# Bucketed attention and a gated expert block on one core: hash masks of 15 of 16 head pairs fetched by bucket number

## Chip, core and metric

One Trainium2 chip, one core. The time is device microseconds of one execution of the whole kernel; the median of the runs shown is given beside the profiled execution's own time.

## Reference

```
q_bits = (einsum('bhsd,dk->bhsk', q, proj) > 0)      # 4 x 8 heads, 768 rows, 64 wide; 6 bits a row
k_bits = (einsum('bhsd,dk->bhsk', k, proj) > 0)
mask   = q_bucket[..., :, None] == k_bucket[..., None, :]   # bucket = the number made of the 6 bits
scores = where(mask, q @ k.T / sqrt(64), -1e9)
attn   = softmax(scores)
x      = (attn @ v), heads side by side: 3072 x 512
out    = (sigmoid(x @ w_gate) * (x @ w_val)) @ w_out        # 512 -> 1536 -> 512
```

A query row attends to those keys of its head whose six hash bits are the same as its own.

## The kernel before

Two heads of one batch make a pair; 16 pairs come one after another (`pair`, `group`). Heads lie on partitions 0 to 63 and 64 to 127, and most products of this stage use the two halves of TensorE's rows side by side. For each pair:

- q and k are loaded by rows, transposed by TensorE (tk, tq), and split into a high and a low fp32r part (`high`, `low`: kh, kl, qh, ql). A copy of the q parts with its halves swapped (qsh, qsl) is made by DMA (`swapped`), so that both heads' queries meet both halves.
- The hash (`hash_`, `hashed`, L1370) multiplies k and q by the projection, six full-array products each (hk, hq). `bits_k` and `bits_q` make 0/1 or large values of the signs: six bits and their six complements a row, in bf16 (kb, qb).
- `group` handles 384 queries of both heads, in three chunks of 128 (t) by two heads (h), so 192 score groups in all. `scores` (L1448, L1454) adds up in PSUM first the bits product qb x kb, two products, which is at least 2^34 smaller wherever a bit differs, and then six products of the q and k parts. The scores are negated, so `maximum` (L1466) is one VectorE reduction that evicts PSUM into the buffer e and keeps the minimum of each row. `exponent` (ScalarE, L1475) makes the exponentials and their sums.
- `turned` transposes e back through TensorE (tp, L1508), `whole` copies it into e again (ScalarE or VectorE, L1514), `values` multiplies by v (pv, L1524), `divided` and `store` finish and write x to DRAM.

Between these pieces run the preparation of the expert weights (`load_w`, `load_pair`: VectorE, ScalarE and GpSimd make high and low parts; SyncE keeps them in DRAM) and the first two of twelve blocks of the expert layer for batches whose attention is done (`moe_early`: zg, zv at L897, zo at L933). When all attention is stored, a switch exchanges the buffers, and the expert stage (`products`) does the rest with weights streamed back by GpSimd's queue.

PSUM has three double banks ("two") for scores, transposes and hashes and two single banks; SBUF has three e buffers. The order is not left to the program text: every step is a task with an engine, a cost in ns, and buffers that it takes and gives (`Plan.add`). For TensorE the table ORDER lists the tasks' numbers in the order in which they are issued; on the other engines the task with the least key goes first among those that are ready, and SHIFT moves the keys. A simulation of the plan with those costs fixes every queue before the kernel is built.

```
    def scores(t, h):
...
            for j, rows in enumerate(halves):
                nc.tensor.matmul(
                    sc[:, j, :GN], z["qb"][rows, c], z["kb"][rows, h], start=True, stop=False, tile_position=(j * D, 0),
                )
```

Of the kernel before, what the change touches and what calls it, by code (L numbers as in the profile page):

```python
# [19 lines left out]
P = 128  # L20
# [5 lines left out]
NEVER = 3.0e38  # L26

# [23 lines left out]
    2, 3, 4, 5, 6, 7, 8, 9, 10, 11, 12, 13, 38, 14, 15, 16, 17, 18, 41, 19, 20, 21, 47, 44, 50, 22, 23, 24, 235, 25,  # L51
    26, 27, 53, 55, 59, 28, 61, 65, 67, 94, 243, 96, 29, 30, 74, 100, 76, 102, 106, 78, 108, 86, 137, 80, 82, 87,
    88, 140, 115, 117, 89, 90, 84, 119, 121, 31, 145, 148, 127, 91, 123, 151, 153, 157, 159, 163, 128, 165, 192,
    194, 198, 125, 129, 172, 238, 174, 130, 131, 200, 176, 204, 206, 178, 333, 132, 184, 185, 336, 213, 246, 341,
    344, 186, 249, 180, 251, 255, 257, 261, 263, 225, 187, 182, 215, 217, 188, 189, 226, 219, 270, 272, 227, 274,
    290, 221, 292, 296, 276, 223, 282, 298, 278, 302, 304, 280, 431, 228, 283, 229, 230, 311, 347, 434, 313, 284,
    285, 315, 349, 353, 355, 359, 442, 439, 361, 317, 323, 324, 286, 325, 287, 368, 388, 319, 370, 380, 390, 321,
    394, 396, 372, 400, 402, 374, 376, 381, 326, 382, 327, 383, 328, 409, 378, 445, 447, 451, 453, 457, 384, 421,
    385, 411, 413, 459, 486, 488, 422, 423, 466, 492, 468, 494, 478, 470, 529, 532, 479, 480, 415, 498, 417, 500,
    419, 472, 424, 425, 426, 481, 507, 627, 509, 1924, 1925, 537, 1926, 1927, 540, 1929, 1930, 635, 1931, 1932, 511,  # L60
    474, 543, 545, 630, 519, 520, 482, 521, 513, 549, 476, 551, 555, 515, 517, 483, 522, 523, 524, 557, 584, 586,
    590, 592, 1934, 1935, 1936, 1937, 638, 1941, 1942, 1943, 564, 566, 596, 598, 568, 576, 570, 641, 572, 1944, 725,
    728, 643, 577, 578, 579, 580, 605, 574, 647, 1948, 607, 649, 653, 655, 1949, 733, 736, 1952, 1953, 609, 662,
    664, 617, 581, 618, 619, 666, 682, 611, 684, 688, 690, 694, 696, 1969, 1970, 1971, 1972, 668, 613, 921, 620,
    621, 615, 703, 705, 1974, 1975, 1976, 1977, 929, 1956, 1957, 707, 709, 711, 622, 715, 716, 674, 717, 713, 670,
    739, 741, 745, 747, 751, 675, 718, 719, 720, 753, 780, 782, 672, 1979, 1980, 1981, 1982, 760, 762, 786, 1986,
    1987, 1988, 1989, 764, 788, 766, 792, 794, 768, 770, 676, 677, 678, 679, 823, 801, 826, 1993, 1994, 831, 1997,
    834, 1998, 803, 805, 807, 813, 809, 837, 811, 839, 843, 845, 849, 851, 924, 814, 815, 816, 817, 818, 858, 878,
    860, 862, 870, 871, 864, 880, 884, 886, 890, 892, 2001, 932, 2002, 866, 868, 1019, 872, 772, 873, 773, 874, 774,
    875, 899, 901, 935, 937, 941, 943, 775, 776, 777, 903, 905, 947, 949, 976, 978, 911, 912, 907, 956, 958, 913,  # L70
    914, 960, 962, 964, 968, 909, 966, 982, 984, 988, 969, 970, 971, 915, 916, 972, 973, 990, 1022, 1117, 2014,
    2015, 2016, 2017, 1027, 2019, 2020, 2021, 2022, 1030, 2024, 1125, 2025, 2026, 2027, 1120, 1033, 1035, 2031,
    2032, 2033, 2034, 1128, 2038, 997, 999, 1039, 1001, 1009, 1003, 1041, 1005, 1007, 2039, 1045, 1047, 1074, 1076,
    1080, 2059, 2060, 2061, 2062, 1054, 1082, 1086, 1088, 1056, 2042, 2043, 1215, 1058, 1218, 1010, 1011, 1012,
# [1595 lines left out]
```

## Time and profile before

| | us |
|---|---|
| median of 3 runs (989.72 to 992.89) | 992.26 |
| the profiled execution's own time | 991.96 |
| its span, first to last instruction | 990.1 |
| TensorE busy in the span | 980.5 |
| VectorE busy | 648.8 |
| ScalarE busy | 546.7 |
| GpSimd busy | 184.7 |
| moved by DMA | 195.96 MB |

Busy times are sums over the whole span, which has two very different stages; the rows below are therefore taken by stage where they can be. TensorE's matmuls are pipelined, so its busy time is no proof that it runs at its peak; the chain of waits tells how long each of its groups took in its place.

### The profile page before, as it was taken

The numbers are of one execution on the slowest core, as the hardware profiler recorded it, in microseconds if no ns is written. First come the engines' busy times: TensorE is split into PE (matmuls) and PEld (weight loads), VectorE is DVE, ScalarE is ACT, GpSimd is POOL, SyncE is SP. The second block draws the span as 40 slices with busy tenths as digits, with TensorE's granted clock in tenths as the row PEclk, the third lists the DMA queues.
The fourth block names the chain that finished last, engine by engine and source line by source line (L and its number), as shares of the span: only waits on it lengthen the run. The fifth ranks groups of instructions, "written<-read, shape, count | busy, mean of one in ns | idle before, by whom it ended". The sixth has DMA issues, their size and how long they took to land.

```text
span 990.1 us, 20196 instructions
## 1 busy us (share of the span) xinstructions
PE 980.5 (99%) x8157; PEld 807.4 (82%) x8160; DVE 648.8 (66%) x1254; ACT 546.7 (55%) x1004; POOL 184.7 (19%) x214
## 2 busy tenths in 40 slices
PE   9999999999998999999999999999999999999998
PEld 5676677777677766776789999999999999999997
DVE  7898989878987888988454775643336433553334
ACT  5768878877767777767645443533234333433331
POOL 1001254343344434341111000000000000000000
PEclk9999999999999999999999999999999999999999
DMA  5375396658686748772279976674447644476421
GB/s 129 92 196 146 122 249 186 196 187 243 196 222 179 242 172 250 216 211 92 66 264 390 385 259 234 236 267 174 180 177 254 237 149 159 170 275 225 149 75 64
DMA packets 115853, 195.96 MB, mean 198 GB/s; under 512 B 62640, under 2 KB 85424, under 8 KB 110640
## 3 DMA queue, kind: packets, MB, share of 16 engines
q1 hardware_dynamic: 107568, 120.68, 40.3%
q0 software_dynamic: 5824, 73.41, 19.9%
q8 instruction: 64, 1.05, 0.4%
q10 hardware_dynamic: 2368, 0.59, 0.3%
q14 instruction: 29, 0.24, 0.1%
HBM read 140.91 MB, written 41.94 MB: 185 GB/s over the span
## 4 chain that ended last, share of the span: by engine, by line
PE 96%; DMA 2%; DVE 1%; ACT 0%; SPq 0%; issue 0%; ACTq 0%; DVEq 0%
PE y L933 17%; PE pv L1524 13%; PE sc L1454 10%; PE zBv L1153 8%; PE zBg L1153 8%; PE tp L1508 8%; PE zDv L1153 4%; PE zDg L1153 4%; PE sc L1448 4%; PE zv L897 4%; PE zo L933 3%; PE zg L897 3%; PE zAg L1153 2%; PE zAv L1153 2%; PE hq L1370 2%; PE hk L1370 1%
## 5 line engine op out<-in xcount | busy, mean ns | idle before, releaser
L1475 ACT ACTIVATE e<-e,st 128x768 f32<-128x768 f32 x192 | 178.8, 933 | 32.4 <-DVE e L1466 31.9
L1466 DVE TENSOR_SCALAR_CACHE_REDUCE e<-sc 128x768 f32<-128x768 f32 x192 | 175.8, 952 | 19.0 <-PE sc L1454 17.2
L933 PE MATMUL y<-wo,gh 128*128 128x512 f32 (+1 forms) x484 | 151.1, 394 | 0.0
L1524 PE MATMUL pv<-e,vr 128*64 128x384 f32 x768 | 137.7, 494 | 0.0
L1514 ACT COPY e<-tp 128x768 f32<-128x768 f32 x126 | 99.1, 798 | 38.2 <-PE tp L1508 37.5
L1508 PEld LDWEIGHTS tp<-ident,e 64*128 64x128 f32 x2304 | 84.6, 139 | 36.6 <-issue 13.9
L933 PEld LDWEIGHTS y<-wo,gh 128*128 128x128 f32 x484 | 90.4, 187 | 15.2
L1508 PE MATMUL tp<-ident,e 64*128 64x64 f32 x2304 | 96.8, 226 | 0.0
L1153 PE MATMUL zBv<-x,wsv 128*128 128x384 f32 x480 | 96.4, 335 | 0.0
L1153 PE MATMUL zBg<-x,wsg 128*128 128x384 f32 x480 | 96.3, 335 | 0.0
L1524 PEld LDWEIGHTS pv<-e,vr 128*64 128x64 f32 x768 | 49.2, 136 | 55.2 <-issue 47.6
L933 PE MATMUL y<-wo,gl 128*128 128x512 f32 (+1 forms) x242 | 93.6, 387 | 0.0
L1454 PE MATMUL sc<-kh,qsl 64*128 64x384 f32 x192 | 89.9, 468 | 2.6 <-DMA qsl<-ql 2.5
L1454 PE MATMUL sc<-kh,ql 64*128 64x384 f32 x192 | 90.0, 469 | 0.0
L1153 PEld LDWEIGHTS zBv<-x,wsv 128*128 128x128 f32 x480 | 85.4, 188 | 5.4 <-ACT t16v L1161 0.2
L1153 PEld LDWEIGHTS zBg<-x,wsg 128*128 128x128 f32 x480 | 85.5, 188 | 5.2
L1246 ACT CAST gh<-zt 128x384 fp32r<-128x384 f32 x80 | 41.0, 514 | 85.8 <-DVE zt L1241 67.6
L1514 DVE COPY e<-tp 128x768 f32<-128x768 f32 x66 | 62.0, 950 | 17.6 <-PE tp L1508 17.3
L1448 PE MATMUL sc<-kb,qb 64*128 64x384 bf16 x384 | 65.0, 328 | 0.1
L1454 PE MATMUL sc<-kl,qh 64*128 64x384 f32 x192 | 64.4, 335 | 0.0
L1454 PE MATMUL sc<-kh,qh 64*128 64x384 f32 x192 | 64.3, 335 | 0.0
L1454 PE MATMUL sc<-kh,qsh 64*128 64x384 f32 x192 | 64.2, 334 | 0.0
(182 smaller groups left out, 1965.7 us busy)
## 6 DMA issues: line engine op xcount, KB each, us to landing
wsg<-kzg POOLq DMA_DIRECT2D x20, 1792.0 KB, 7.8
wsv<-kzv POOLq DMA_DIRECT2D x20, 1792.0 KB, 7.6
kzg<-wkg SPq DMA_DIRECT2D x10, 896.0 KB
kzv<-wkv SPq DMA_DIRECT2D x10, 896.0 KB
vr<-in_v_dram SPq DMA_DIRECT2D x16, 384.0 KB
rb<-rd SPq DMA_DIRECT2D x64, 96.0 KB
xd<-xs SPq DMA_DIRECT2D x32, 192.0 KB
rawg<-in_moe_w_gate_dram SPq DMA_DIRECT2D x12, 512.0 KB
```

The costliest lines, as they stand in the source:

```text
L897: nc.tensor.matmul(z["acc"][:, :GN], a[:, wc], x[xx][:, c, :], start=(c == 0 and i == 0), stop=(c == KC - 1 and i == 2),)
L933: nc.tensor.matmul(acc, a[:, slot, ts_], w, start=(first and i == 0), stop=(last and i == 2), skip_group_check=cols != slice(None),)
L1153: nc.tensor.matmul(acc, streams[n, jp][:, c, wa, a_], X[x_][:, xa, c], start=first and c == 0 and i == 0, stop=c == 1 and i == 2, skip_gro ...
L1246: nc.scalar.copy(side["h"][:, blk], w["z", blk])
L1370: nc.tensor.matmul(acc[:, j, :GN], hw[w][a], z[n + x][:, j * GN : (j + 1) * GN], start=m == 0, stop=m == 2,)
L1448: nc.tensor.matmul(sc[:, j, :GN], z["qb"][rows, c], z["kb"][rows, h], start=True, stop=False, tile_position=(j * D, 0),)
L1454: nc.tensor.matmul(sc[:, j, :GN], q_[rows, c], z["k" + x][rows, h * GN : (h + 1) * GN], start=False, stop=(m == 2), tile_position=(j * D, 0),)
L1466: nc.vector.tensor_scalar(sp(e), gz["sc", t, h][:, :, :GN], -MASKED * SCALE, None, op0=ALU.min, op1=ALU.min, accum_out=gz["st", t][:, h : ...
L1475: nc.scalar.activation(e, e, AF.Exp, bias=st[:, h : h + 1], scale=-1.0, accum_out=gz["su"][:, h * GT + t : h * GT + t + 1],)
L1508: nc.tensor.transpose(tp[:, r, at_ : at_ + D], gz["e", t, h][rows, c * P : (c + 1) * P], ident[rows, rows], tile_position=(r * D, 0),)
L1514: copy(gz["e"][:, :, c * P : (c + 1) * P].rearrange("p n (r d) -> p r n d", r=2), gz["tp", c][:, :, :GN].rearrange("p r (n d) -> p r n d", ...
L1524: nc.tensor.matmul(gz["pv"][rows, :GN], z["v"][:, h, c], gz["e"][:, h * GT : (h + 1) * GT, c * P : (c + 1) * P], start=(c == 0), stop=(c = ...
```

## The change

For all pairs but the first, the bits product leaves the score groups. Instead:

- `bits` makes the 12 sign bits of k, and `differ` multiplies them by a table `code` of all 64 bucket numbers (built once from `blank`, `digits`, `code_turned`, `coded`): four bf16 products per pair give, for each of 64 buckets and each key of a head, how many bits differ. `masks` turns this into 0 or 2^60 in bf16, and `keep_masks` writes it to DRAM: 128 rows (two heads by 64 buckets) of 768.
- `hash_q` computes the six hash values of each query with queries on the partitions (24 small products: a 128-query weight and 12 or 6 columns), and `buckets` turns them into a bucket number by three small VectorE instructions.
- `gather`, an indirect DMA on GpSimd's queue, fetches for each query row the mask row of its bucket, into the upper half of that chunk's place in e: 12 per pair, 180 in all, 196,608 bytes each. The six gathers of a group now take the e buffer.
- `maximum` becomes a reduction with two inputs (scores from PSUM, mask from SBUF), which adds and keeps the minimum.
- hash bits of the first pair, its bits product and its reduction stay as they were.
- ORDER and SHIFT are new tables; one line of each:

```
-    2, 3, 4, 5, 6, 7, 8, 9, 10, 11, 12, 13, 38, 14, 15, 16, 17, 18, 41, 19, 20, 21, 47, 44, 50, 22, 23, 24, 235, 25,
+    7, 8, 9, 10, 11, 12, 13, 14, 15, 16, 17, 18, 43, 19, 20, 21, 22, 46, 23, 52, 49, 24, 5, 25, 55, 26, 27, 142, 58,
```

```diff
+DIRECT = (0,)
...
+    GATHER, GATHERED, AHEAD, EARLY = 1250, 5200, 8, 4
...
+        def bits():
+            z["kb"] = at.tile([P, 2, GN], BF16, name=f"kb{u}", tag="kb", bufs=1)
+            nc.vector.tensor_scalar(z["kb"], z["hs", "k"][:, :, :GN], own, None, op0=ALU.is_gt)
+
+        def differ():
+            for h in range(2):
+                for j, rows in enumerate(halves):
+                    nc.tensor.matmul(
+                        z["hs", "k"][:, j, :GN], code[rows, h], z["kb"][rows, h], start=h == 0, stop=h == 1,
+                        tile_position=(j * D, 0),
+                    )
+
+        def masks():
+            z["tb"] = at.tile([P, S], BF16, name=f"tb{u}", tag="tb", bufs=1)
+            nc.vector.tensor_scalar(sp(z["tb"]), z["hs", "k"][:, :, :GN], 1.0, OTHER, op0=ALU.min, op1=ALU.mult)
+
+        def keep_masks():
+            nc.sync.dma_start(td[i], z["tb"])
+
+        def hash_q():
...
+            for m in range(NC):
+                c = slice(m * P, (m + 1) * P)
+                for a in ("h", "l"):
+                    for h, rows in enumerate(halves):
+                        high = a == "h"
+                        nc.tensor.matmul(
+                            to[:, h, :, m] if high else to[:, h, 0, m], z["q" + a][rows, c],
+                            hw_q[rows] if high else hw_q[rows, 1], start=high, stop=not high,
+                            tile_position=(h * D, 0), skip_group_check=True,
+                        )
+
+        def buckets():
...
+            nc.vector.tensor_reduce(qd.rearrange("p (h m) r -> p h (m r)", h=2), both, axis=AX.X, op=ALU.add)
+            nc.vector.scalar_tensor_tensor(
+                qw, qd, 0.0, power.unsqueeze(1).broadcast_to([P, 2 * NC, NB]), op0=ALU.is_gt, op1=ALU.mult,
+            )
...
+                nc.vector.tensor_reduce(z["id"], qw, axis=AX.X, op=ALU.add)
...
+                for a in swaps:
+                    a.slack = 2500
...
+        def gather(t, h):
...
+            gz["m", t, h] = m = gz["e"][:, h * GT + t].bitcast(BF16)[:, S:]
+            at_ = h * NC + g * GT + t
+            nc.gpsimd.indirect_dma_start(
+                m, None, td[i], bass.IndirectOffsetOnAxis(ap=z["id"][:, at_ : at_ + 1], axis=0), element_offset=h * D * S,
+            )
...
-            for j, rows in enumerate(halves):
+            for j, rows in enumerate(halves if direct else []):
...
+            if i not in DIRECT:
+                nc.vector.tensor_tensor_reduce(
+                    sp(e), gz["sc", t, h][:, :, :GN], sp(gz["m", t, h]), 1.0, NEVER, ALU.add, ALU.min, gz["st", t][:, h : h + 1],
+                )
+                return
...
+                masked[t, h] = add(
+                    t0 + t + h * 0.5 - AHEAD, "pool", GATHER, lambda t=t, h=h: gather(t, h), after=found,
+                    take=["e"] * (h == 0 and t == 0), tail=GATHERED, size=196608, behind=[masked[0, 0]] if h or t else [],
+                )
```

How the instructions move shows best on TensorE where the second batch's first scores follow the last value product whose e buffer they will use. (Names: sc scores, tp transposes of e, pv value product; the numbers are the pair's place in its batch, the group, and for sc the chunk and the head.) Before:

```order
L1524 MATMUL pv_2_1_1708<-e_2_1_1355,vr_2_1061 64x384 x2
L1508 MATMUL tp_3_1_0_1939<-ident,e_3_1_1773 128x64 x12
L1508 MATMUL tp_3_0_5_1956<-ident,e_3_0_1576 128x64 x12
L1448 LDWEIGHTS qb_0_1680
L1448 MATMUL sc_0_0_0_0_1971<-kb_0_1692,qb_0_1680 128x384
L1448 LDWEIGHTS qb_0_1680
L1448 MATMUL sc_0_0_0_0_1971<-kb_0_1692,qb_0_1680 128x384
L1454 MATMUL sc_0_0_0_0_1971<-kh_0_1498,ql_0_1579 128x384
L1454 MATMUL sc_0_0_0_0_1971<-kh_0_1498,qsl_0_1655 128x384
L1454 MATMUL sc_0_0_0_0_1971<-kl_0_1499,qh_0_1578 128x384
L1454 MATMUL sc_0_0_0_0_1971<-kl_0_1499,qsh_0_1617 128x384
L1454 MATMUL sc_0_0_0_0_1971<-kh_0_1498,qh_0_1578 128x384
```

Between `pv_2_1` and the scores `sc_0_0_0_0` stand 24 transposes. In the order of the change, at the same place:

```order
L1595 MATMUL sc_3_1_2_1_2012<-kl_3_1131,qh_3_1231 128x384
L1595 MATMUL sc_3_1_2_1_2012<-kh_3_1130,qsh_3_1340 128x384
L1595 MATMUL sc_3_1_2_1_2012<-kh_3_1130,qh_3_1231 128x384
L1654 MATMUL tp_3_0_3_2020<-ident,e_3_0_1500 128x64 x12
L1401 MATMUL tk_1_2034<-ident,kr_1_1593 128x64 x12
L1670 MATMUL pv_3_0_2049<-e_3_0_1500,vr_3_1485 64x384 x6
L1595 MATMUL sc_0_0_0_0_2070<-kh_0_1590,ql_0_1754 128x384
L1595 MATMUL sc_0_0_0_0_2070<-kh_0_1590,qsl_0_1866 128x384
L1595 MATMUL sc_0_0_0_0_2070<-kl_0_1591,qh_0_1753 128x384
L1595 MATMUL sc_0_0_0_0_2070<-kl_0_1591,qsh_0_1833 128x384
L1595 MATMUL sc_0_0_0_0_2070<-kh_0_1590,qh_0_1753 128x384
L1595 MATMUL sc_0_0_0_0_2070<-kh_0_1590,qsh_0_1833 128x384
```

Here the last piece of `pv_2_1` stands further up: between it and these scores come three score groups, 24 transposes of e, 12 of k (tk) and a piece of another value product. The scores have lost their loads of qb and two products, and begin with a product of fp32r parts right behind a value product. Over the whole program TensorE goes to scores from a value product or a full-array product 52 times (15 before), to value products 85 times (62), to full-array products 50 times (36), and to transposes from those two kinds 65 times (78).

GpSimd's queue of before, from the first step of weight preparation that the new order has among gathers (mf, ex: parts of expert weights):

```order
L715 TENSOR_TENSOR mfv_1933<-mfv_1933,exv_1924 128x512
L771 TENSOR_TENSOR we<-mfv_1933,we 128x512
L715 TENSOR_TENSOR mfo_2123<-mfo_2123,exo_2112 128x512
L871 TENSOR_TENSOR xl_0_2260<-xr_0_2121,xh_0_2259 128x384
L771 TENSOR_TENSOR wo_2291<-mfo_2123,wo_2291 128x512
L871 TENSOR_TENSOR xl_0_2260<-xr_0_2121,xh_0_2259 128x384 x3
L715 TENSOR_TENSOR mfg_1_2352<-mfg_1_2352,exg_1_2347 128x512
```

And that of the change (the rows with td are the gathers of one group, e the buffer that they fill, id the bucket numbers):

```order
L779 TENSOR_TENSOR mfv_1870<-mfv_1870,exv_1837 128x512
L835 TENSOR_TENSOR we<-mfv_1870,we 128x512
L1577 DMA e_0_0_1981<-td_102,id_0_1855 128x768 x6
L779 TENSOR_TENSOR mfo_2079<-mfo_2079,exo_2064 128x512
L1577 DMA e_0_1_2175<-td_102,id_0_1855 128x768 x5
L835 TENSOR_TENSOR wo_2177<-mfo_2079,wo_2177 128x512
L1577 DMA e_0_1_2175<-td_102,id_0_1855 128x768
L779 TENSOR_TENSOR mfo_2376<-mfo_2376,exo_2356 128x512
L1577 DMA e_1_0_2451<-td_103,id_1_2228 128x768
L935 TENSOR_TENSOR xl_0_2471<-xr_0_2324,xh_0_2470 128x384
L1577 DMA e_1_0_2451<-td_103,id_1_2228 128x768 x2
L835 TENSOR_TENSOR wo_2497<-mfo_2376,wo_2497 128x512
```

The gathers stand between the weights' steps, six to a group, and a weight step behind a gather waits for that gather's buffer too. Over the whole program 10 of 16 sets of sums (four additions each), 7 low parts of weight pairs, 10 of x and 5 of gated blocks have moved from GpSimd to VectorE; 19 copies of e and 4 high parts have moved from VectorE to ScalarE.

## Rows read from the trace of the kernel before

**Rows 1.** By window: length, busy PE, PEld, DVE, ACT, POOL; PEclk, DMA share, GB/s.

```profile
0.00:512.00 512.00, 506.18 (x5677) 367.00 (x5680) 421.62 (x853) 372.58 (x674) 160.75 (x173) 1.00 0.63 181
0.00:450.00 450.00, 445.47 (x5061) 321.88 (x5066) 387.14 (x787) 338.07 (x610) 150.53 (x163) 1.00 0.67 190
```

**Rows 2.** The chain of waits, 0 to 512 us, shares by line.

```profile
by line: PE pv L1524 25.9%; PE sc L1454 19.8%; PE tp L1508 15.6%; PE sc L1448 7.1%; PE zv L897 6.0%; PE zg L897 5.3%; PE zo L933 4.5%; PE hq L1370 3.0%; PE hk L1370 2.8%; DMA qsl<-ql 2.4%; PE tq L1331 1.2%; PE tk L1331 1.2%; DMA qr<-in_q_dr
```

**Rows 3.** Pieces of that chain in order: start us, us, what.

```profile
205.31 0.90 PE tp L1508 x24
206.21 0.16 PE sc L1448 x2
206.37 0.53 PE sc L1454 x6
206.90 0.18 PE sc L1448 x2
...
209.70 2.73 PE pv L1524 x16
212.43 0.27 PE sc L1448 x2
...
222.34 0.37 PE tp L1508 x12
...
245.75 0.52 PE tp L1508 x12
...
247.80 1.44 PE pv L1524 x8
```

**Rows 4.** The same near the end of the stage.

```profile
495.97 2.30 PE zg L897 x12
...
499.66 2.08 PE zg L897 x12
```

**Rows 5.** VectorE's groups, 0 to 512 us: count, busy us, mean ns, idle before.

```profile
L1466 DVE TENSOR_SCALAR_CACHE_REDUCE e<-sc 128x768 f32<-128x768 f32 x192 | 175.8, 952 | 19.0 <-PE sc L1454 17.2
L1514 DVE COPY e<-tp 128x768 f32<-128x768 f32 x66 | 62.0, 950 | 17.6 <-PE tp L1508 17.3
L1388 DVE TENSOR_SCALAR kb<-hk,thr_k 128x384 bf16<-128x384 f32 x32 | 18.4, 610 | 5.4 <-PE hk L1370 5.2
L1531 DVE TENSOR_TENSOR xs<-pv,rb 128x384 f32<-128x384 f32 x32 | 17.7, 552 | 12.7 <-PE pv L1524 12.7
L1381 DVE TENSOR_SCALAR qb<-hq,thr_q,mul_q 128x768 bf16<-128x768 f32 x16 | 17.2, 1073 | 4.2 <-PE hq L1370 4.2
...
L1466 DVE DVE_READ_ACCUMULATOR e<-sc 128x1 f32 x192 | 15.8, 82 | 0.0
L1357 DVE TENSOR_TENSOR kl<-tk,kh 128x768 fp32r<-128x768 f32 x16 | 15.2, 948 | 1.7 <-ACT kh L1345 1.6
```

**Rows 6.** GpSimd's groups, 0 to 512 us.

```profile
L833 POOL TENSOR_TENSOR wkg<-mfg,wkg 128x896 fp32r<-128x896 f32 x8 | 16.9, 2110 | 10.8 <-ACT wkg L830 10.8
...
L572 POOL DMA_DIRECT2D praw<-in_proj_dram x2 | 1.2, 600 | 0.8 <-POOLq L1654 0.8
```

**Rows 7.** DMA queues (first row 0 to 450 us, others whole span) and issues, landing last.

```profile
q1 hardware_dynamic: 88413, 84.13, 65.5%
...
q0 software_dynamic: 5824, 73.41, 19.9%
...
wsg<-kzg POOLq DMA_DIRECT2D x20, 1792.0 KB, 7.8
...
praw<-in_proj_dram POOLq DMA_DIRECT2D x2, 1.5 KB, 3.4
```

**Rows 8.** A late transfer: a stretch of full DMA engines, the wait, the stretch behind.

```profile
125.00:150.00 25.00, 24.95 (x304) 19.78 (x304) 21.34 (x41) 18.51 (x34) 14.32 (x16) 1.00 1.01 256
...
300.00:325.00 25.00, 25.00 (x277) 20.21 (x277) 21.74 (x44) 20.68 (x40) 12.21 (x13) 0.93 0.55 163
...
299.79 0.44 PE L1454 MATMUL sc<-kh,qsl 64*128 64x384 f32 x1 [2.53 <-DMA qsl<-ql]
```

More of the change, by code (lines that the diff above doesn't have):

```diff
@@ L26 @@
 NEVER = 3.0e38
+OTHER = float(2**60)
+DIRECT = (0,)
 SEEN = {"pe": 0, "act": 150, "pool": 85, "dve": 125, "sp": 0}
@@ L1291, in lsh_attention_glu_kernel @@
     add(-10.5, "act", 1300, lambda: None)
+    a = add(-5, "pool", 2000, blank)
+    a = add(-5, "dve", 1300, digits, after=[a])
+    parts_q_ = add(-5, "pool", 700, parts_q, after=[a])
+    b = add(-4, "pe", 250, code_turned, after=[a], take=["one"])
+    coded_ = add(-4, "dve", 350, coded, after=[b], give=["one"])
     def pair(i):
@@ new lines, in buckets @@
+        def buckets():
+            qd, qw = (at.tile([P, 2 * NC, NB], F32, name=f"{x}{u}", tag=x, bufs=1) for x in ("qd", "qw"))
+            z["id"] = at.tile([P, 2 * NC], U32, name=f"id{u}", tag="id", bufs=2)
+            both = z["hs", "q"][:, :, : NC * 2 * NB].rearrange("p h (a n) -> p h n a", a=2)
+            nc.vector.tensor_reduce(qd.rearrange("p (h m) r -> p h (m r)", h=2), both, axis=AX.X, op=ALU.add)
+            nc.vector.scalar_tensor_tensor(
+                qw, qd, 0.0, power.unsqueeze(1).broadcast_to([P, 2 * NC, NB]), op0=ALU.is_gt, op1=ALU.mult,
+            )
+            with nc.allow_low_precision(reason="sums of six powers of two, whole numbers below 64"):
+                nc.vector.tensor_reduce(z["id"], qw, axis=AX.X, op=ALU.add)
@@ L1415, in pair @@
                 swaps = [add(n_, "sp", 1200, lambda x=x: swapped(x), after=[y], tail=2000, size=3.0e5) for x, y in (("h", a), ("l", needs[1]))]
+                for a in swaps:
+                    a.slack = 2500
         if i == 0:
             first_loads.append(last_turn)
-        for m, n in enumerate("kq"):
+        found = []
+        if i not in DIRECT:
+            n_ = t0 - 2.8 - EARLY
+            a = add(n_, "pe", 6 * MM, lambda: hash_("k"), after=[needs[0]], take=["two"])
+            a = add(n_, "dve", 870, bits, after=[a])
+            a = add(n_, "pe", 2 * MM + 8, differ, after=[a, coded_], kind="scores")
+            a = add(n_, "dve", 870, masks, after=[a], give=["two"])
+            kept_masks = add(n_, "sp", 600, keep_masks, after=[a], tail=2500, size=196608)
+            n_ += 0.6
+            a = add(n_, "pe", NC * 2 * TH, hash_q, after=[needs[1], parts_q_], take=["two"], kind="turn")
+            found = [add(n_, "dve", 560, buckets, after=[a], give=["two"]), kept_masks]
+            z["second"] = None
+        for m, n in enumerate("kq" if i in DIRECT else ""):
             n_ = t0 - 2.8 + m * 0.6
@@ L1541, in group @@
                 a = score_tasks[n] = add(
-                    n + h * 0.5, "pe", 4 * MM + 8, lambda t=t, h=h: scores(t, h), after=[x for x in needs if h or x is not z["second"]] + score_tasks.get("last", []),
-                    take=["two"] + ["e"] * (h == 0 and t == 0) + ["st"] * (h == 0), kind="scores",
+                    n + h * 0.5, "pe", (4 if i in DIRECT else 3) * MM + 8, lambda t=t, h=h: scores(t, h), after=[x for x in needs if h or x is not z["second"]] + score_tasks.get("last", []),
+                    take=["two"] + ["e"] * (h == 0 and t == 0 and not found) + ["st"] * (h == 0), kind="scores",
                     give=["h"] if g == NG - 1 and t == GT - 1 and h == 1 else [],
@@ L1546, in group @@
                 score_tasks["last"] = [a]
-                least.append(add(n - 3, "dve", 878, lambda t=t, h=h: maximum(t, h), after=[a], give=["two"]))
+                least.append(add(n - 3, "dve", 878, lambda t=t, h=h: maximum(t, h), after=[a, masked.get((t, h))], give=["two"]))
             for h in range(2):
```

54 lines of the change are left out of this document (48 added, 6 removed), and 646 rows, old and new, of tables (ORDER, SHIFT).

## The prediction

> **What bounds the kernel now.** I read the table by stage first. The attention stage fills the first 512 us of the 990.1, the expert stage the other 478. In the first, TensorE is busy 506 of 512 us, VectorE 422, ScalarE 373, GpSimd 161 [rows 1]. The change leaves the expert stage's work alone, so only the 512 us are in play. A busy TensorE is not yet a TensorE with no slack, so the next view is the chain of waits cut to that stage: TensorE's own groups take nearly all of it, and one DMA, the swapped query copy qsl, 2.4% [rows 2]. The mask products, which the change removes for 15 pairs, are 7.1% of 512 us, 36.4 us for 192 score groups, 0.189 us each. The pieces in order of time show what a group costs where it stands: inside a run, 0.18 us for the mask products and 0.53 for the six others; after transposes 0.16; after a value product 0.27 [rows 3]. So entering scores from a value product costs 0.09 more; I read it as the load of a first, narrow bf16 weight that nothing hides. Twelve transposes take 0.37 us after scores and 0.52 after a value product, so entering with an fp32 weight from another array layout costs 0.15; from scores, whose layout is the same, nothing [rows 3]. Value products take 1.44 us for 8 and 2.73 for 16, so 0.16 each and 0.15 for the entry [rows 3]. Twelve full-array products take 2.08 us where they follow their own kind and 2.30 after something else: entry 0.2 [rows 4].
>
> **TensorE, term by term.** (a) 180 mask pairs go: 180 x 0.189 = **-34.0 us**.
> (b) Scores now begin with an fp32 weight. By the order, TensorE enters scores from value or full-array products 52 times instead of 15. At 0.15 each that is +7.8; the 15 old entries are already in the 0.189. Entries from transposes are taken at nothing, because the reverse change costs nothing [rows 3]. Bounds 0 and 52 x 0.3 = 15.6.
> (c) Query hash: 3.0% of 512 is 15.4 us for 16 pairs [rows 2], so 15 pairs give back 14.4. In their place stand 24 small products per pair, each a weight load with 6 or 12 columns. No row shows this; the nearest is a transpose, also one load and few columns, 0.37 us for 12 [rows 3], so 24 take 0.75 and 15 pairs 11.2. Net -3.2, with -14.4 (nothing at all) as the lower and +8 (twice the transposes' price) as the upper bound.
> (d) The code products, four bf16 products per pair, cost twice a mask pair, 0.36 us and some entries: 15 x 0.41 = +6.2.
> (e) The new order is cut into smaller pieces. Value products are entered 85 times instead of 62 (+3.5 at 0.15), full-array ones 50 instead of 36 (+2.8 at 0.2), transposes from those kinds 65 instead of 78 (-2.0): +4.3.
> Sum: -34.0 + 7.8 - 3.2 + 6.2 + 4.3 = **-18.9 us**, with bounds -38 (b and c at their lower ends) and 0 (both at their upper ends).
>
> **VectorE** has 387 us of work in its dense 450 us [rows 1], so its load decides whether TensorE can use that. Two bit rows (2 x 0.61, 1.07) become two 768-wide ones (about 1.07 each): -34.4 + 32.2 us over 15 pairs [rows 5]. Two-input instructions fit 0.156 us plus 1.03 ns per element (552 ns at 384, 948 at 768 [rows 5]); the three bucket instructions (288 elements) then add 15 x 0.77 = 11.5. The order moves 40 additions of 128, 7 of 896 and 15 of 384 elements from GpSimd to VectorE, +27.4; 19 copies and 4 high parts go to ScalarE, 23 x 0.95 = -21.9 [rows 5]. Setup adds some 2. Sum +17. The reduction itself changes kind, to one that adds the fetched mask while it takes the minimum. The trace of before has no such instruction. A one-input reduction of this size takes 952 ns with 82 for its accumulator; adding two inputs, PSUM and SBUF, without a reduction, takes 948 [rows 5]. I take 0.95, so no change, with a lower bound of -0.08 (no accumulator read) and an upper bound of +0.95 (two passes). VectorE's dense stretch then holds 404 us of work in 450 - 18.9 = 431, 94%. It hides, but with 27 us to spare, 0.15 us per reduction. ScalarE gains at most 22 us on 338 [rows 1], 84% of 431: hidden.
>
> **GpSimd and the DMA engines.** GpSimd loses about 50 us of arithmetic (7 x 2.11 is the largest part [rows 6]) and gets 180 gathers. Lower bound for one: 0.60, its plain DMA issue; upper: 2.11, its longest instruction there [rows 6]. I take 1.0, nearer to the plain DMA: 161 - 50 + 180 = 291 us of 493, hidden, and at the upper bound 491, no longer. The gathers fetch 180 x 196,608 B = 35.4 MB and the 15 kept tables add 2.9. Packets of the hardware queue cost 65.5% of 450 x 16 us for 84.1 MB, 56 us per MB; the software queue's large ones 43 (19.9% of 990 x 16 for 73.4) [rows 7]. So 38.3 MB cost 1,650 to 2,150 us, 103 to 134 on each of 16 engines. On 0.67 x 450 = 301 us [rows 1] that makes 404 to 435 us of 431: the DMA engines are nearly full. Before, stretches at a share of 1.01 did not hold TensorE (24.95 of 25 us busy), but a late qsl held it once for 2.5 us, with the granted clock at a mean of 0.93, part of the stretch on the lower of its two levels, in the 25 us behind it [rows 8].
> The row says only that each share is high; the Trainium skill, page "DMA: Bandwidth & Descriptors", section "Issuing engines are not separate DMA queues", says that DMAs started on different engines run on the same 16 engines and interleave, which speaks against this change. By it every gather lengthens the loads of SyncE's queue, and the sum would go from -18.9 to the price of the first rival; no run here shows it yet.
>
> **What is late next.** A gather writes into the buffer that its scores will later overwrite, so it starts only when the last value product of three groups earlier has read it; before, that hand-over needed no transfer. By the order and the durations of rows 2 to 4, the work TensorE has between that moment and the end of the first score is 4.2 us at least and 7.4 in the middle of 29 hand-overs; before it was as little as 0.7. A gather should land about 3.9 us after its issue: the two loads of GpSimd took 3.4 us for 1.5 KB and 7.8 for 1,792 KB [rows 7], so 192 KB add 0.5. If nothing slows it, no hand-over waits; at 6 us seven do, 7 us in all; at 8 us nineteen, 31 us. The vector instruction that waits for a gather also holds up the copies and evictions queued behind it on VectorE, and TensorE has three double banks to run ahead. I put +4 us in. The kept tables pass through SyncE's queue behind the masks; their hashes stand some groups earlier in the order, so I cost them at nothing.
> **Sum:** 991.96 of the profiled execution (span 990.1 and 1.9 around it) - 18.9 + 4 = **977 us**. The median shown, 992.26, is 0.3 higher; I don't correct for it.
>
> **Rivals.**
> 1. *Gathers land late.* With the DMA engines near full, landings stretch to 8 us. TensorE waits 31 us over the hand-overs: 992 - 19 + 31 = **1,004**. It decides from a landing of about 7.2 us, where the waits reach 18.5 us and eat the gain. For it: the share of 94 to 101%, and the clock after a wait. Against: a plain 1,792 KB load needs only 7.8 us. Chance 0.22.
> 2. *VectorE becomes the bound.* If the new reduction costs 0.25 us more, 45 us go on top of 404, 18 over the 431: 977 + 18 = **995**, at 0.2 us **986**. For it: VectorE is at 94%. Against: 948 ns for the same two inputs. Chance 0.11.
> 3. *Entries are free.* If first weights load under the preceding product wherever they stand, (b) and (e) vanish and the late qsl goes too: 977 - 12 - 4 = **961**. For it: entering transposes from scores costs nothing [rows 3]. Against: 0.15 after value products [rows 3]. The Trainium skill, page "TensorE: Matmul & The Clock Gate", section "Step-by-step: what each phase is for", says that TensorE pulls weight loads ahead of running matmuls where row groups don't conflict or the background buffer is the target; the trace agrees inside one layout and not across layouts. Chance 0.12.
>
> **How the numbers follow.** The forecast has 0.55, its own range 967 to 987. Faster by over 0.3%, about what a measurement of this kernel can tell from no change: 0.55 + 0.12 + 0.02 of rival 2 = 0.69. Slower: rival 1 but for 0.03, and 0.03 of rival 2: 0.22. Within 0.3%: 0.09. The range runs from rival 3 to rival 1, 962 to 1,004; outside lie half of rival 1 and half of rival 3.
>
> **What would show it.** Right: the score line's share of the chain falls to its six products, the mask line keeps 12 groups; the attention stage ends near 497; VectorE's first 430 us are some 94% busy; the new reduction takes 0.95; few waits of VectorE for DMA. Wrong: long idle time of the reduction or of TensorE behind gathers, landings over 7 us, a reduction of 1.1 us or more, or an attention stage that ends after 508 with TensorE full.

## The result and the profile after

| | before | after |
|---|---|---|
| median of 4 executions each (lowest to highest), us | 992.2 (989.7 to 992.9) | 1,002.6 (999.6 to 1,006.0) |
| ratio, with its 95% interval | | 1.011 (1.0065 to 1.0155) |
| the profiled execution / its span | 991.96 / 990.1 | 1,005.17 / 1,003.4 |
| TensorE busy in the span | 980.5 | 983.2 |
| VectorE / ScalarE / GpSimd busy | 648.8 / 546.7 / 184.7 | 668.3 / 565.0 / 314.4 |
| moved by DMA, MB | 195.96 | 234.35 |

The change made the kernel 1.1% slower; the prediction was 977. The table by stretches of the changed kernel, with the columns of [rows 1]:

```profile
0.00:512.00 512.00, 497.74 (x5586) 349.57 (x5590) 434.51 (x928) 385.25 (x686) 285.65 (x297) 0.99 0.83 249
0.00:450.00 450.00, 435.77 (x4890) 306.13 (x4894) 392.12 (x842) 342.54 (x609) 259.19 (x272) 0.99 0.87 260
450.00:530.00 80.00, 77.75 (x780) 57.77 (x779) 53.30 (x99) 52.49 (x96) 33.59 (x32) 1.00 0.59 192
```

The first stage did not get shorter: it ends some 13 us later, and the expert stage behind it takes as long as before. TensorE is busy 435.77 of the first 450 us, where it was busy 445.47 [rows 1]: it now waits. GpSimd's load and the DMA share have risen. The chain of waits, 0 to 530 us, shares by line, and five long pieces of it (start, us, what), to be held against [rows 2]:

```profile
by line: PE pv L1670 19.0%; PE sc L1595 13.9%; PE tp L1654 11.1%; DMA e<-td,id 8.1%; PE zv L961 5.1%; issue 5.1%; PE zg L961 4.0%; PE hq L1488 3.3%; PE zo L997 3.3%; PE hk L1440 2.6%; DMA td<-tb 2.1%; DVE e L1608 1.9%; DVE e L1612 1.4%; POO
...
47.05 7.56 DMA e<-td,id
249.26 8.27 DMA e<-td,id
287.15 7.16 DMA e<-td,id
324.10 7.34 DMA e<-td,id
386.61 11.15 DMA td<-tb
```

The mask line is gone from the head of the list, and the fetches (e<-td,id) stand there with 8.1% of 530, 43 us; the store of a table (td<-tb) comes once with 11. A piece of the chain is not yet lost time, since TensorE has work of its own beside many of them. What the unit prices are, is in the groups of VectorE, GpSimd and TensorE (columns as in [rows 5]):

```profile
L1608 DVE CUSTOM_DVE_ANT_0 e<-sc,e 128x768 f32<-128x768 f32 x180 | 169.1, 952 | 17.9 <-PE sc L1595 10.7 <-DMA e<-td,id 6.4
L1608 DVE DVE_READ_ACCUMULATOR2_ANT st<- 128x1 f32 x180 | 14.9, 83 | 0.0
L1500 DVE SCALAR_TENSOR_TENSOR qw<-qd,power 128x72 f32<-128x72 f32 x15 | 6.2, 412 | 1.0 <-DVE qd L1499 0.5
L1577 POOL DMA_INDIRECT e<-td,id x180 | 178.6, 992 | 128.0 <-issue 44.7 <-PE sc L1595 23.8 <-ACT e L1621 11.6
```

The reduction with two inputs takes 952 ns, as the one-input one did [rows 5], and a fetch 992 ns of GpSimd: both are what the prediction took. The error is elsewhere, and the pieces of the chain of the changed kernel show where TensorE's part of it lies:

```profile
230.84 1.44 PE pv L1670 x8
232.28 0.73 PE sc L1595 x6
...
260.08 1.50 PE hq L1488 x24
261.58 1.16 PE sc L1595 x12
...
265.54 0.37 PE tp L1654 x12
265.91 0.58 PE sc L1595 x6
```

A score group of six products takes 0.58 after transposes, and 0.73 after a value product. Before, a group with its mask products took 0.16 + 0.53 = 0.69 and 0.27 + 0.53 = 0.80 there [rows 3]. So the removed products, priced at 0.189, gave back 0.11 and 0.07 us at these places. The hash of a pair's queries takes 1.50 for its 24 small products, twice the 0.75 forecast.

To see the whole of it, I sorted the time up to the expert stage by the start times of TensorE's products, over the traces of all kernels here: **products**, at the interval they keep inside a run of their kind (six score products 0.51, a pair of mask products 0.175, a small product of the new hash 0.056); **entries**, the usual extra time of a run, by its kind and the kind ahead (the median over the runs of all kernels here but one that is set apart below); **waits**, what a run takes beyond that; and the **lower clock**, half the time on the lower of the two levels. The idle products that fill the start are left out.

| us | products | entries | waits | lower clock |
|---|---|---|---|---|
| before | 465.7 | 38.6 | 8.3 | 1.7 |
| after | 443.4 | 61.4 | 19.7 | 3.3 |

The products fell by 22.3 us, since those of the new hash and of the code table took back 25.0 of the 47.3 that the mask products and the old hash had taken. Entries rose by 22.8, waits by 11.4, the lower clock by 1.6: 13.5 in all, against 13.3 between the spans. How the time divides between the first three columns depends on the intervals taken, by about 1 us. Score groups stand in 137 runs instead of 85, and entering them costs 21.6 instead of 7.0.

### The profile page after: what moved, and what is told of

It reads as the page before. It is cut to its first block, busy times and chain, and to the rows that moved or that the text cites. A ratio compares the mean times of both kernels' runs of the same rounds, so it can differ in the third digit from the quotient of the medians.

```text
span 1003.4 us, 20840 instructions
## 1 busy us (share of the span) xinstructions
PE 983.2 (98%) x8129; PEld 801.0 (80%) x8132; DVE 668.3 (67%) x1337; ACT 565.0 (56%) x1027; POOL 314.4 (31%) x342
## 2 busy tenths in 40 slices
DMA packets 129538, 234.35 MB, mean 234 GB/s; under 512 B 65760, under 2 KB 90464, under 8 KB 124320
## 4 chain that ended last, share of the span: by engine, by line
PE 82%; DMA 7%; DVE 5%; issue 3%; POOL 2%; ACT 1%; SPq 0%; DVEq 0%; ACTq 0%; POOLq 0%
PE y L997 17%; PE pv L1670 10%; PE zBv L1217 8%; PE zBg L1217 8%; PE sc L1595 7%; PE tp L1654 6%; DMA e<-td,id 4%; PE zDv L1217 4%; PE zDg L1217 4%; PE zv L961 3%; PE zo L997 2%; PE zg L961 2%; PE zAg L1217 2%; PE zAv L1217 2%; PE hq L1488 2%
## 5 line engine op out<-in xcount | busy, mean ns | idle before, releaser
L1577 POOL DMA_INDIRECT e<-td,id x180 | 178.6, 992 | 128.0 <-issue 44.7
L1608 DVE CUSTOM_DVE_ANT_0 e<-sc,e 128x768 f32<-128x768 f32 x180 | 169.1, 952 | 17.9 <-PE sc L1595 10.7
L1670 PE MATMUL pv<-e,vr 128*64 128x384 f32 x768 | 143.1, 498 | 0.4 <-DVE e L1660 0.4
L1660 ACT COPY e<-tp 128x768 f32<-128x768 f32 x145 | 113.7, 797 | 43.9 <-PE tp L1654 41.8
L1654 PEld LDWEIGHTS tp<-ident,e 64*128 64x128 f32 x2304 | 87.1, 139 | 37.5 <-issue 17.9
L1654 PE MATMUL tp<-ident,e 64*128 64x64 f32 x2304 | 99.0, 226 | 3.1 <-DVE st L1608 2.8
L1595 PE MATMUL sc<-kh,ql 64*128 64x384 f32 x192 | 79.3, 413 | 1.7 <-DVE st L1608 0.8
L1595 PE MATMUL sc<-kh,qsl 64*128 64x384 f32 x192 | 79.4, 414 | 1.1 <-ACT e L1660 0.9
L1774 POOL DMA_DIRECT2D wsg<-kzg x20 | 10.6, 532 | 206.6 <-PE zDv L1217 163.1
L1774 POOL DMA_DIRECT2D wsv<-kzv x20 | 10.8, 542 | 197.9 <-PE zDg L1217 187.9
```

The source lines that it names most:

```text
L1577: nc.gpsimd.indirect_dma_start(m, None, td[i], bass.IndirectOffsetOnAxis(ap=z["id"][:, at_ : at_ + 1], axis=0), element_offset=h * D * S,)
L1595: nc.tensor.matmul(sc[:, j, :GN], q_[rows, c], z["k" + x][rows, h * GN : (h + 1) * GN], start=not direct and m == 0, stop=(m == 2), tile_p ...
L1608: nc.vector.tensor_tensor_reduce(sp(e), gz["sc", t, h][:, :, :GN], sp(gz["m", t, h]), 1.0, NEVER, ALU.add, ALU.min, gz["st", t][:, h : h + 1],
L1654: nc.tensor.transpose(tp[:, r, at_ : at_ + D], gz["e", t, h][rows, c * P : (c + 1) * P], ident[rows, rows], tile_position=(r * D, 0),)
L1660: copy(gz["e"][:, :, c * P : (c + 1) * P].rearrange("p n (r d) -> p r n d", r=2), gz["tp", c][:, :, :GN].rearrange("p r (n d) -> p r n d", ...
L1670: nc.tensor.matmul(gz["pv"][rows, :GN], z["v"][:, h, c], gz["e"][:, h * GT : (h + 1) * GT, c * P : (c + 1) * P], start=(c == 0), stop=(c = ...
```

## Experiments

Two theories were tried. By the theory of **entries**, what the mask products cost is mostly given back as first weight loads of an order cut into shorter runs. By the theory of **fetches**, the fetched masks come late and TensorE waits for VectorE, which waits for them. Ratios are to the kernel before, in the same set of runs.

### 1. The old order without its mask products

```diff
-            for j, rows in enumerate(halves):
+            for j, rows in enumerate([] if i else halves):
                 nc.tensor.matmul(sc[:, j, :GN], z["qb"][rows, c], z["kb"][rows, h], ...
...
-                        start=False, stop=(m == 2), ...
+                        start=bool(i) and m == 0, stop=(m == 2), ...
```

> The kernel before, in its old order, but the score groups of pairs 1 to 15 leave out their two bits products (the hash and the bits are still made, nothing masks the scores). It prices term (a) and the entry of term (b) by themselves. Theory of entries: a group in a run gets 0.18 us shorter, but each of the 85 runs of score groups then begins with an fp32 weight load that costs some 0.11 us more; 180 x 0.175 - 80 x 0.11 = 23 us off: 969 us, ratio 0.977. Rival, flat price as in the prediction: 34 off, 958, ratio 0.966. Second rival, the loads of weights bound the six products and the bits products lay in their shadow: 15 off or less, 977 or more.

Measured 988.7, ratio 0.9958 (0.9946 to 0.997): 4 us, not 23. That lies in the span of the second rival, but not by its mechanism: inside the run below the six products still take 0.52 a group, as they did beside the bits products (0.53 [rows 3]), so these did not lie in the shadow of weight loads. The sorted time gives products 434.2 (31.5 less, at those intervals), entries 46.6 (8.0 up, as the theory had it) and waits 25.0 instead of 8.3; some 11 of the 17 us of new waits stand in the 20 of the 85 runs that have four or five groups. One run of five groups, TensorE and then VectorE by time (start, us, instruction; a group's first product each, one row of two that start together):

```profile
151.29 0.44 PE L1454 MATMUL sc<-kh,qsl 64*128 64x384 f32 x1
...
151.92 0.34 PE L1454 MATMUL sc<-kh,qsl 64*128 64x384 f32 x1
...
152.44 0.33 PE L1454 MATMUL sc<-kh,qsl 64*128 64x384 f32 x1
...
153.15 0.44 PE L1454 MATMUL sc<-kh,ql 64*128 64x384 f32 x1
...
154.03 0.44 PE L1454 MATMUL sc<-kh,qsl 64*128 64x384 f32 x1
```

```profile
152.13 0.96 DVE L1466 TENSOR_SCALAR_CACHE_REDUCE e<-sc 128x768 f32<-128x768 f32 x1 [0.16 <-PE sc L1454]
153.01 0.08 DVE L1466 DVE_READ_ACCUMULATOR e<-sc 128x1 f32 x1
...
153.89 0.08 DVE L1466 DVE_READ_ACCUMULATOR e<-sc 128x1 f32 x1
```

The first three groups stand 0.52 to 0.63 apart. The fourth starts at 153.15, 0.14 behind the end of the first reduction's pass at 153.01, and the fifth at 154.03, 0.14 behind the second's at 153.89. The three double banks are full, and the run goes on at VectorE's pace, 0.88 a group.

### 2. Is it VectorE's pace? The same with a shorter reduction

```diff
+            n = GN // 2 if i else GN
-                sp(e), gz["sc", t, h][:, :, :GN], ...
+                sp(e[:, GN:] if i else e), gz["sc", t, h][:, :, :n], ...
```

> The old order without bits products in pairs 1 to 15 (the first experiment), and the reduction, the exponential and the transposes read only half of the score columns there, so a reduction takes about 0.55 us instead of 0.95 and gives its double bank back sooner; TensorE's products are all kept. If the first experiment's 16 us of excess came from runs of four and five score groups that catch up with VectorE's reductions over three double banks, they go: 988.7 - 13 to 16 = 973 to 976, and the groups of a run stand 0.52 us apart throughout. If the excess is TensorE's own (weight loads), nothing changes: 987 to 989.

Measured 974.8, ratio 0.9817 (0.9799 to 0.9836): as the theory of banks had it. Its mean reduction is 579 ns over 192 (12 of them at full length), and a run of five groups, the last product's end included:

```profile
146.37 2.83 PE sc L1454 x30
```

That is 0.57 a group; in the first experiment five took 3.46 (151.29 to the next kind at 154.75). The exponential got shorter here too, so ScalarE could have a part in it. The idle time of TensorE's weight loads ahead of scores, by what ended it (us, times, longest), tells the two apart. First experiment:

```profile
PEld sc L1454 <- DVE e L1466: 11.5, 31, 0.6
PEld sc L1454 <- ACT e L1514: 6.6, 25, 0.4
```

This one:

```profile
PEld sc L1454 <- ACT e L1515: 5.8, 24, 0.3
PEld sc L1454 <- DVE e L1467: 1.5, 3, 0.6
```

The waits for reductions went, those for ScalarE's copies of transposes stayed. So mask products in a long run lay in the shadow of VectorE's reductions. The new order has only 2 runs of more than three groups among its 137; its short runs are the other way out, and they pay in entries.

### 3. The removed products put back into the new order

```diff
+            for j, rows in enumerate([] if direct else halves):
+                nc.tensor.matmul(
+                    sc[:, j, :GN], code[rows, h], later["kb0"][rows, h], start=True, stop=False, tile_position=(j * D, 0),
+                )
```

> The changed kernel with two bf16 products (the code table by the first pair's bits, a stand-in that adds small whole numbers to the scores) put ahead of each score group of pairs 1 to 15, everything else as changed. If entries with an fp32 weight cost 0.11 us and a bf16 pair that stands first takes that cost away, the 180 pairs add 180 x 0.175 = 31.5 and give back 125 entries x 0.11 = 14, and some of the waits for fetches vanish behind the longer TensorE work: 10 to 18 us more than the changed kernel, 1,013 to 1,020. If a pair has the flat price of 0.189, 34 more: 1,036.

Measured 1,014.1, ratio 1.0214 (1.0201 to 1.0227): 10 to 12 us above the changed kernel's ratios, not 34. The sorted time: products 31.5 up, entries 9.7 down, waits 13.5 down. So a bf16 pair in front costs 0.06 us of time where its products take 0.175: of the rest, some 0.05 is the entry that it makes cheaper (9.7 us over 180 groups), and some 0.08 are waits that vanish behind the longer work (13.5).

### 4. Without the fetches

```diff
-            nc.gpsimd.indirect_dma_start(
-                m, None, td[i], bass.IndirectOffsetOnAxis(...), element_offset=h * D * S,
-            )
...
-            if i not in DIRECT:
-                nc.vector.tensor_tensor_reduce(...)
-                return
```

> The changed kernel without the 180 fetches: the reduction of pairs 1 to 15 is the one-input one of the first pair, nothing masks their scores; masks, bucket numbers and all TensorE work stay. Theory of entries: only the waits go, 18 us of excess over TensorE's usual intervals against 7 before, so 8 to 11 us off: 991 to 995. Rival, the fetches are the cause of the whole loss against the forecast: 25 off, 977. Rival, the waits come from elsewhere (order, start): 1,000 or more.

Measured 992.5, ratio 1.0004 (0.9992 to 1.0016). Waits fall to 8.8, what they were before, and the clock stays on its higher level throughout. This splits the error in two: the fetches cost some 8 to 10 us, and everything else in the change comes to nothing gained (-0.1) where -18.9 was forecast.

### 5. Fetches of few bytes

```diff
-    td = [dram.tile([P, S], BF16, ...
+    td = [dram.tile([P, D], BF16, ...
...
-            gz["m", t, h] = m = gz["e"][:, h * GT + t].bitcast(BF16)[:, S:]
+            gz["m", t, h] = m = gz["e"][:, h * GT + t].bitcast(BF16)[:, S : S + D]
```

> The changed kernel with fetches of 64 columns instead of 768 (128 rows of 128 bytes, stores of the masks as narrow), into the same place of e, so every wait and every instruction of GpSimd stays and 92 per cent of the fetched bytes go; the reduction adds another bf16 tile. If the load on the DMA engines makes the fetches late, this gains as much as leaving them out: 991 to 995. If the hand-over of e and GpSimd's pace of 1.25 us a fetch do, it gains 0 to 3 us: 1,000 to 1,003.

Measured 995.9, ratio 1.0031 (1.002 to 1.0041): between the two answers. Some 6 to 8 of the 8 to 10 us go with the bytes (those of the fetches and of the stores of the masks, which are narrow here too), and 3.4 stay. In this trace no reduction waits for a fetch any more, so the 3.4 come by another way; whether by the hand-over of e or by GpSimd's pace is not shown. The stretch of 0 to 450 us shows what the bytes were, a DMA share of 0.68 instead of 0.87 with GpSimd as busy as before:

```profile
0.00:450.00 450.00, 442.26 (x5018) 311.23 (x5020) 401.06 (x861) 349.82 (x623) 262.86 (x277) 1.00 0.68 194
```

### 6. The price of the small products

```diff
-                for a in ("h", "l"):
+                for a in ("h",):
...
-                            ..., start=high, stop=not high,
+                            ..., start=True, stop=True,
```

Three kernels have this edit: one without fetches, one with thin ones, one with all. The first:

> The changed kernel without fetches and with 12 small products: nothing masks the scores of pairs 1 to 15. If TensorE's own intervals set the time once the fetches are gone, the two gains add up: 992.5 - 10 = 982 to 984. If VectorE, which has 435 us in 512, then holds TensorE through the double banks, half of the gain is lost: 986 to 989.

Measured 984.6, ratio 0.9917 (0.99 to 0.9933): 7.9 off, nearer to the first answer. The hash's runs fall from 20.1 to 11.1 us by the start times, 0.050 for each product left out. With thin fetches:

> Fetches of 64 columns as in the fourth experiment and 12 small products. If the late signals come with the fetched bytes, they are gone: 995.9 - 8 = 987 to 989. If they come with GpSimd's issue of the fetches, which is unchanged here, 1,100 or more.

Measured 990.1, ratio 0.9973 (0.9956 to 0.9989): 5.8 off. With all fetches, first:

> The changed kernel with 12 instead of 24 small products in the hash of the queries: those with the low parts are left out (bucket numbers may differ where a hash is near zero). If a small product costs what its fp32 weight load leaves exposed, 0.056 us as the intervals between them show, 15 x 12 x 0.056 = 10 us go: 992 to 994. If it costs what a transpose does (0.031, the price in the prediction), 5.6 go: 997. If TensorE is held by the fetches anyway, 0 to 2 go: 1,001 or more.

It took a median of 1,134.5 over six executions (1,129.2 to 1,139.4), which nothing above explains. So the changed kernel was run again, and this one too:

> The changed kernel once more, unaltered, beside the three kernels that follow, so that they have it on their own chip: 1,000 to 1,006, ratio 1.008 to 1.014.

Measured 1,001.7, ratio 1.0089 (1.0058 to 1.012).

> The kernel with 12 small products and all fetches, which took 1,134 in place of the 992 to 997 expected, once more. There the trace shows consumers starting up to 6.7 us after the product they wait for has ended, during bursts of fetches. If it belongs to the kernel, 1,130 to 1,140 again; if it was a state of that chip, 992 to 997.

Measured 1,000.6, ratio 1.0073 (1.0038 to 1.0108): not 1,134, so the edit alone does not bring that time on. The changed kernel was not in the set that had it, so whether it would have been slow there too is not known. And once more, with more executions:

> 12 small products and all fetches, with more executions than the two before, which gave 1,134 and 1,000.6. If the fetches hold TensorE, so that time taken from its products comes back as waits, 999 to 1,002, ratio 1.006 to 1.009. If TensorE's products set the time in spite of them, 8 less than the changed kernel, 993 to 994, ratio 1.001. If the late signals come up again, 1,060 or more.

Measured 1,000.8, ratio 1.008 (1.0058 to 1.0103), as the first answer had it. With all fetches the saving is hardly there. The hash's runs are 9 us shorter here too, but the waits outside them are 25 to 27 us, where the changed kernel has 17 to 20; without fetches they go from 9 to 10 only. Half of the edit:

```diff
-                for a in ("h", "l"):
+                for a in ("h", "l")[: 1 + (m < GT)]:
```

> The changed kernel with 18 small products: the low parts of the last three query chunks are left out. By the price of a small product 5 us less than the changed kernel: 996 to 999. If fewer small products by themselves call up the late signals, 1,060 or more.

Measured 998.6, ratio 1.0059 (1.0034 to 1.0083): 3 us less than the changed kernel beside it and inside the 996 to 999 expected, but with an interval that also holds the ratios of the two kernels with 12, so it does not stand apart from them. Those two show it: with full fetches, 10 us taken from TensorE's products gave 1 to 4 us of time, and the rest came back as waits.

No kernel here that keeps the masks beats the kernel before. Even with thin fetches, which mask nothing, and with half the hash this design only comes to 990.1.

## Why the prediction was wrong, by its own steps

The prediction named the right places, and its unit prices on VectorE, GpSimd and the code products held. Its sum of TensorE's terms, -18.9, was measured by the fourth experiment as -0.1, the upper end of its own bounds, and its +4 of waits as +8 to +10. Times by the start times of the products, after less before; (a) is 180 times the interval of a pair inside a run, and what else its place was worth stands in (b):

| step | forecast | measured |
|---|---|---|
| (a) 180 mask pairs | -34.0 | -31.5 |
| (b) entries to scores | +7.8 | +14.6 |
| (c) query hash: old out / new in | -14.4 / +11.2 | -15.8 / +19.9 |
| (d) code products | +6.2 | +5.1 |
| (e) other entries, with turns and setup | +4.3 | +8.4 |
| new waits, lower clock | +4 | +13.0; +7 in the changed kernel's second profile (1,000.2) |

By size, the waits were off by 9.0 (3 in the second profile), (c) by 7.3, (b) by 6.8, (e) by 4.1, (a) by 2.5 and (d) by 1.1 the other way.

- **(b) failed at the step "Entries from transposes are taken at nothing, because the reverse change costs nothing".** The price of one direction was used for the other. The 71 entries to scores from other kinds cost some 9 us, near the forecast. The 66 from transposes of e or of q and k cost some 0.2 each, 13 in all; before, with a bf16 product at the head of the run, 68 of them cost some 0.1 each, 7 in all. An fp32 weight load now comes first, and the third experiment, which puts a bf16 pair ahead of it, takes 9.7 us of entries off. The timeline of the entry behind the small products (261.44 to 261.70 for the first pair of products, then every 0.17 to 0.18; one row of each pair):

```profile
261.44 0.42 PE L1595 MATMUL sc<-kh,ql 64*128 64x384 f32 x1
...
261.70 0.33 PE L1595 MATMUL sc<-kl,qh 64*128 64x384 f32 x1
...
261.88 0.33 PE L1595 MATMUL sc<-kh,qh 64*128 64x384 f32 x1
...
262.05 0.33 PE L1595 MATMUL sc<-kh,qsl 64*128 64x384 f32 x1
```

The load of a bf16 weight is shown with 95 ns, that of an fp32 one with 186 to 188 (the first row before, the others after; 100 to 500 us):

```profile
L1448 PEld LDWEIGHTS <-qb 64*128 64x128 bf16 x294 | 16.2, 95 | 17.9 <-issue 14.6
...
L1595 PEld LDWEIGHTS sc<-kl,qsh 64*128 64x128 f32 x151 | 28.1, 186 | 0.0
L1488 PEld LDWEIGHTS hq<-hw_q,ql 64*128 64x128 f32 x132 | 13.2, 188 | 0.0
```

The Trainium skill, page "TensorE: Matmul & The Clock Gate", section "Weight-path perf modes — Fast Weight Load (FWL) and DoubleRow", says that 128 weights load fast unless their type is FP32; the trace agrees (95 against 186 to 188). The mask products were the fast entry of each run as well as a cost, and the third experiment shows both.
- **(c) was priced by the wrong neighbour.** A transpose was taken as the nearest row, and gave 0.031 each; a small fp32r product costs 0.056. Two of them, on the two halves of the rows, go side by side every 0.111 us:

```profile
261.11 0.25 PE L1488 MATMUL hq<-hw_q,ql 64*128 64x6 f32 x2
261.22 0.26 PE L1488 MATMUL hq<-hw_q,qh 64*128 64x12 f32 x2
261.33 0.25 PE L1488 MATMUL hq<-hw_q,ql 64*128 64x6 f32 x2
```

The Trainium skill, page "TensorE: Matmul & The Clock Gate", section "LDWEIGHTS (loading the stationary operand)", gives a load as its columns divided by 1.2 in ns, whatever the number of rows; for these 128 columns that is an estimate of 107 ns. The 111 ns between two starts agree with it, the 188 ns that the profile shows for one load do not. Two transposes, with as many columns of weights, start every 0.06 us, below that estimate too, which is why they were the wrong neighbour. At 19.9 us the new hash costs more than the 15.8 it replaces.
- **The waits** have the mechanism of rival 1, at a smaller size. The step that failed is "A gather should land about 3.9 us after its issue", which was worked out from two loads that are not fetches. For its reader a fetch has landed when the last completion signal has come in on its semaphore. By that the 180 fetches landed 5.4 us after their start (median; 9.7 at most), and 24 of them took longer than the 7.2 from which rival 1 decides; with the narrow rows of the fifth experiment the median is 3.8. Nine times VectorE stood idle before a reduction until a fetch had landed (us in all, times, longest):

```profile
DVE e L1608 <- DMA e<-td,id: 6.4, 9, 1.7
```

One of them waited for the fetch that starts at 47.05, the fourth of its group, whose 7.56 us stand in the chain above. GpSimd issues a fetch every 1.25 us (0.95 and a pause of 0.30), and the reduction begins when this one has landed:

```profile
47.05 0.95 POOL L1577 DMA_INDIRECT e<-td,id  x1 [0.30 <-issue]
48.30 0.94 POOL L1577 DMA_INDIRECT e<-td,id  x1 [0.30 <-issue]
49.55 0.95 POOL L1577 DMA_INDIRECT e<-td,id  x1 [0.30 <-issue]
```

```profile
54.74 0.96 DVE L1608 CUSTOM_DVE_ANT_0 e<-sc,e 128x768 f32<-128x768 f32 x1 [0.38 <-DMA e<-td,id]
```

The pace of six fetches a group, 6.3 us from the first to the last at the least, did not make the last ones late: from landing to reduction the sixth of a group had 6.5 us to spare (median), the first 2.7. TensorE's longest wait began with a second step that failed, the kept tables, of which the prediction said "so I cost them at nothing". GpSimd stood for 10.9 us until a table was stored, the piece of 386.61 in the chain:

```profile
POOL e L1577 <- DMA td<-tb: 10.9, 1, 10.9
```

Two other profiles with full fetches have it too (11.3 and 10.2, the kernel with half the hash); the changed kernel's second one has not. How such a wait reaches TensorE stands in the chain and in TensorE's timeline at 400 us: the fetches behind that store start at 398.53, one from 401.86 holds the reduction until 408.59, and a hash behind it on TensorE waits for its double bank:

```profile
401.86 6.60 DMA e<-td,id
...
408.59 0.14 DVE e L1608
```

```profile
409.61 0.44 PE L1440 MATMUL hk<-kh,hw_l 128*128 128x384 f32 x1 [2.64 <-DVE st L1608]
```

TensorE's granted clock is at a mean of 0.93 in the 25 us around this wait, so part of them were on the lower of its two levels, 1.2 GHz:

```profile
400.00:425.00 25.00, 22.15 (x221) 17.64 (x217) 18.72 (x40) 15.71 (x27) 13.76 (x14) 0.93 0.87 256
```

- **The DMA engines** are at 0.87 of 450 us, 392 us each, below the 404 to 435 of the forecast. That transfers of all queues share the DMA engines, which the prediction took from the Trainium skill, page "DMA: Bandwidth & Descriptors", section "Issuing engines are not separate DMA queues", against this change, the fifth experiment bears out: some 6 to 8 us go when the bytes go.
- **VectorE** stayed in bounds on average, 392 of 450 us, and rival 2 did not come. But "its load decides whether TensorE can use that" was the wrong question. In a run of more than three score groups it is VectorE's pace that counts, 0.88 a group, and the first experiment shows that without the masks the old order would have gained 4 us. The prediction named the three double banks and did not hold 0.53 a group against 0.95 a reduction. With 2 such runs left in the new order, this is not where its 25 us went; it says why the price of the masks could not be had in the old order either.
- **Rival 3**, free entries, fell by the trace: entering scores costs 21.6 us, not nothing. That the time landed near rival 1's 1,004 is a coincidence: late fetches made only some 10 us of it, and the 31 us that rival 1 put on them did not come.

What would have given a better forecast from the rows at hand: 34 us is the price of the masks where they stand in the chain. A group without them goes at the pace of its reduction in long runs, and costs an fp32 entry in short ones.

## To carry to other kernels

Before pricing a cut in the work of a producer, hold its interval inside a burst against the interval of what empties its buffers: beyond the number of buffers the run goes at the slower pace (here 0.88 us a group instead of 0.52), whatever the average load says. A cheap instruction at the head of a run may also be the cheap way into it; price the entry that will take its place, in the direction in which it will be made. A transfer that becomes part of a hand-over is priced to the signal that lets its reader start, and with the load that it brings itself: here 5.4 us in the median, with a tail to 9.7, where 3.9 had been taken from other transfers.

## What the runs showed of the hardware that was not expected

- A fetch of 128 rows by a list of indices costs GpSimd 0.95 to 0.99 us and a pause of 0.30, whether the rows have 128 or 1,536 bytes. To its last completion signal it takes 3.8 us in the median with the narrow rows (DMA share 0.68), 5.4 with the wide ones (0.87).
- In the one set of runs in which the kernel with half the hash took 1,134 us, 23 copies of transposes by ScalarE and VectorE began 1.1 to 5.4 us after both their transposes and their engine were free, each within 2.8 us of the start of a fetch, and TensorE's clock had a mean of 0.946; in the changed kernel's profile no such copy is later than 0.1 us. ScalarE's copy of transposes that ended at 132.08 in the chain began at 136.29 (start, us, instruction, idle before and what ended it):

```profile
136.29 0.80 ACT L1660 COPY e<-tp 128x768 f32<-128x768 f32 x1 [3.67 <-remote]
```

and TensorE, which needed that bank, stood still:

```profile
132.08 5.07 issue
```

Kernels without fetches in the same set took 974.8 and 984.6, near what was expected of them, and the same kernel took 1,000.6 and 1,000.8 in two later sets. What brings this on stays open.
